# Attention decode step with an MLP on one core: unread products in TensorE's waits, half of the last matrix as 512-column products, three weight loads fewer, no VectorE branch

## The chip, the core and the metric

The kernel runs on one core of a Trainium2 chip. The metric is the device time of one execution in microseconds. Three runs of the kernel before took 190.09 to 190.26 us, with a median of 190.16 us.

## What is computed

One token goes through grouped-query attention over a cache of 16384 positions (32 query heads, 8 key/value heads, head size 128), then through a block that ends in an MLP of width 1792. The shifts that the block applies along the sequence have a sequence of length one, so `jnp.pad` and the slices leave zeros, `hs` is zero and `x1` is the block's own input.

```python
x = A_x                                            # (1, 1, 512), bfloat16 like all inputs
q = layernorm(x) @ wq                              # 512 -> 32 heads x 128
scores = einsum("bhqd,bhkd->bhqk", q, k) * 128 ** -0.5   # k, v: 8 heads, each used by 4 query heads
o = einsum("bhqk,bhkd->bhqd", softmax(scores), v)
h = x + o.reshape(1, 1, 4096) @ wo                 # 4096 -> 512
z = layernorm(h)
x1 = z                                             # z + hs, with hs = 0
h2 = h + x1 + gelu(layernorm(x1) @ w3) @ w4        # 512 -> 1792 -> 512
```

Keys and values are 32 MB each (counted in 1024s), wq and wo 4 MB each, w3 and w4 1.75 MB each: 79.17 MB in all are read from memory.

## The kernel before

**Recording and issuing.** The kernel is recorded as a list of operations for each engine (`Program.op`), with the keys that each reads and writes; `emit` turns dependences into semaphore waits and issues each engine's list. ScalarE, GpSimd and SyncE are issued in straight order by `_run`. TensorE's list is issued by `_tensor`, which turns the repeated parts (queries, keys, values of the four pairs of heads) into loops with registers and branches. Each engine works its list strictly in this order. An operation recorded with no function (`dve(None)`, `pe(None, ...)`) marks a place: there `_vector` and `_tensor` put a branch that is never taken, with a prefetch hint placed at the start of the engine's program (lines 144 and 150 for VectorE, 219 and 317 for TensorE). On TensorE the mark stands before w4's sixth chunk and carries the wait for the second half of `hcol`.

**Loads.** All large loads are issued by SyncE through one queue, at line 438, in order: wq, keys of pair 0 in two halves, values of pair 0, keys of pair 1, and so on. Each later one waits until its buffer is free. The keys of a pair go into two buffers `kb[0]` and `kb[1]`, the values into `vb`; the last pair's values are two loads. After the last keys, `kb[0]` takes wo and `kb[1]` takes w3 and w4. The constants `WO`, `W3` and `W4` cut these into separate loads, each with its own semaphore: wo into three (24, 6 and 2 of its 32 columns of blocks), w3 into two (3 and 1 of 4 chunks), w4 into four (5, 5, 3 and 1 of 14 chunks).

**One pair of heads.** VectorE transposes keys from `kb` to `kt` (line 590), TensorE multiplies them with the query (lines 601 and 607), VectorE finds the maximum (617, 618), TensorE averages it (620), ScalarE takes the exponential (628), VectorE transposes the probabilities into `pt` (632), TensorE sums the denominators (650) and multiplies 64 times with the values, 512 columns each (643), VectorE gathers the blocks into `od` (659, 662) and TensorE adds them up (665).

**The tail.** After the fourth pair, in order:

- 32 products of the attention output with wo, 512 columns each (709). The weights are 32 columns wide, so four products work side by side in four column groups of the array. Their sum in PSUM is copied to `osum` in SBUF (713), and four fp32 products with `row32` add its partitions up into the residual row (715).
- Row sums for the layernorm (487 to 499, with TensorE's product at 497); ScalarE makes `hc` (721). `hc` waits for the first piece of w3.
- 16 products with w3, 448 columns each (727); variance and the power on GpSimd (505 to 513); `xsum` (732); ScalarE's Gelu in two halves (736); VectorE transposes each half to `hcol` (740).
- One fp32 product that puts `xsum` into the output sums `n_ps` (744), then 14 chunks of w4, each as four products of 128 columns into the four partition groups of `n_ps` (751): 56 products.
- ScalarE and VectorE copy the result to `fin` (756, 758), SyncE stores it (759).

## Time and profile before

| what | value |
|---|---|
| median of three runs | 190.16 us |
| the profiled execution's own time | 190.25 us |
| its span | 188.9 us |
| mean granted TensorE clock over the span | 0.819 of full speed |
| read from memory | 79.17 MB |

The span runs from the first to the last instruction of the core; the execution's own time includes what lies around it, 1.35 us here. PE stands for TensorE's products, PEld for its weight loads, DVE for VectorE, ACT for ScalarE, POOL for GpSimd and SP for SyncE; SPq is SyncE as issuer of loads. L709 is line 709 of the kernel before. Times in a row are microseconds from the span's start; in brackets stands how long the engine was idle before the row, and what ended that wait. The columns of other views are told where they are shown.

### The profile page before, as it was taken

What the parts mean: (1) busy time and instruction counts of PE and PEld (TensorE: products, weight loads), DVE (VectorE), ACT (ScalarE), POOL (GpSimd) and SP (SyncE); (2) the same over time, 40 slices, a digit from 0 to 9 for tenths busy, and PEclk for the clock granted to TensorE, in tenths of its full rate; (3) what the DMA queues carried; (4) which work ended last, traced back from release to release, by engine and by line L of the source; (5) the groups of instructions that cost most, each with busy time, mean ns of one, the idle gap of its engine ahead of it and who ended that gap; (6) DMA issues with size and microseconds to landing.
All of it is one profiled execution on the core that took longest, in us unless ns stands there. A gap on an engine that the chain in (4) does not pass through costs nothing.

```text
span 188.9 us, 2164 instructions
## 1 busy us (share of the span) xinstructions
PE 117.9 (62%) x695; PEld 46.2 (24%) x695; DVE 115.3 (61%) x140; ACT 9.3 (5%) x16; POOL 5.9 (3%) x11
## 2 busy tenths in 40 slices
PE   1009808998176399950832999606639997185664
PEld 1003303332032134320300333202213332031232
DVE  4900699995522999945047989460269897513252
ACT  3000000000200000002000000020000000500011
POOL 1900000000000000000000000000000000000010
PEclk9999996999657669996695699965797999558675
DMA  6999999999799999997999999997999999999994
GB/s 222 444 444 444 444 444 444 444 444 444 333 444 444 444 555 444 430 402 333 416 416 444 444 444 444 444 444 333 444 444 444 444 444 409 430 409 416 416 403 184
DMA packets 3325, 79.19 MB, mean 419 GB/s; under 512 B 378, under 2 KB 508, under 8 KB 1276
## 3 DMA queue, kind: packets, MB, share of 16 engines
q1 hardware_dynamic: 3316, 79.17, 98.0%
q8 instruction: 1, 0.02, 0.0%
q10 hardware_dynamic: 8, 0.00, 0.0%
HBM read 79.17 MB, written 0.00 MB: 419 GB/s over the span
## 4 chain that ended last, share of the span: by engine, by line
DMA 66%; DVE 18%; PE 10%; issue 4%; SPq 1%; DVEq 0%
DMA kb<-in_A_k_cache_dram 45%; DVE kt L590 16%; DMA kb<-in_B_w_dram 14%; DMA vb<-in_A_wq_dram 6%; PE banks L567 5%; PE banks L607 5%; SPq L438 1%; DVE qcol L574 1%; DVE qb L581 0%; PE banks L751 0%; PE banks L601 0%; DVE xn L558 0%; DVE fin L758 0%; SPq L137 0%; DVEq L137 0%
## 5 line engine op out<-in xcount | busy, mean ns | idle before, releaser
L590 DVE STREAM_TRANSPOSE kt<-kb 128x2048 int32<-128x2048 int32 (+1 forms) x37 | 71.3, 1987 | 4.7 <-DMA kb<-in_A_k_cache_dram 3.8
L607 PE MATMUL banks<-kt,qn 128*128 x256 | 68.5, 411 | 0.5
L607 PEld LDWEIGHTS banks<-kt,qn 128*128 x256 | 26.0, 102 | 41.2 <-issue 25.4
L643 PE MATMUL banks<-vb,pt 128*32 128x512 bf16 x256 | 23.9, 555 | 3.0 <-POOLq L453 3.0
L659 DVE TENSOR_SCALAR od<-banks,rowc 128x128 f32<-128x128 f32 x4 | 1.4, 350 | 26.0 <-PE banks L643 26.0
L567 PE MATMUL banks<-vb,xn 128*128 x32 | 9.2, 461 | 9.7 <-DVE xn L558 9.7
L601 PE MATMUL banks<-qn 128*128 128x512 bf16 x8 | 3.7, 468 | 18.0 <-DVE kt L590 17.9
L632 DVE STREAM_TRANSPOSE pt<-p_sb 64x1024 bf16<-64x1024 bf16 x8 | 9.9, 1239 | 5.4 <-ACT p_sb L628 5.3
L643 PEld LDWEIGHTS banks<-vb,pt 128*32 128x32 bf16 x256 | 8.8, 134 | 16.3 <-issue 11.9
L628 ACT ACTIVATE p_sb<-banks,bias 128x1024 bf16<-128x1024 f32 x4 | 4.5, 1114 | 155.6 <-DVE nmh L624 155.6
L650 PE MATMUL banks<-acc,zd 128*32 128x1 f32 x8 | 1.1, 201 | 17.7 <-DVE pt L632 17.7
L617 DVE TENSOR_REDUCE mx<-banks 128x1 f32<-128x1024 f32 x4 | 4.9, 1224 | 8.1 <-PE banks L607 8.1
L574 DVE STREAM_TRANSPOSE qcol<-banks 64x1024 f32<-64x1024 f32 x4 | 4.8, 1227 | 7.3 <-PE banks L567 7.3
L567 PEld LDWEIGHTS banks<-vb,xn 128*128 128x128 bf16 x32 | 3.7, 115 | 14.9 <-issue 12.6
L513 POOL TENSOR_TENSOR st<-st,expo 128x1 f32<-128x1 f32 (+1 forms) x2 | 1.3, 632 | 175.8 <-DVE st L511 175.8
L620 PE MATMUL banks<-mxd,mean 128*128 128x128 f32 x8 | 2.0, 326 | 6.6 <-DVE mxd L618 6.6
L601 PEld LDWEIGHTS banks<-qn 128*128 128x128 bf16 x8 | 0.8, 99 | 20.9 <-issue 20.8
L665 PE MATMUL banks<-od,zo 128*32 128x128 f32 x8 | 1.6, 285 | 6.5 <-DVE od L662 6.5
L650 PEld LDWEIGHTS banks<-acc,zd 128*32 128x32 f32 x8 | 0.7, 138 | 18.4 <-DVE pt L632 18.4
L662 DVE SCALAR_TENSOR_TENSOR od<-banks,rowc,od 128x128 f32<-128x128 f32 x12 | 4.2, 351 | 0.4
L709 PE MATMUL banks<-kb,o_b 128*32 128x512 bf16 x32 | 3.3, 583 | 1.3 <-DMA kb<-in_A_wo_dram 1.3
L555 DVE COPY zo<-rowgh 128x32 f32<-128x32 f32 x1 | 3.6, 3630 | 0.0
(72 smaller groups left out, 43.2 us busy)
## 6 DMA issues: line engine op xcount, KB each, us to landing
kb<-in_A_k_cache_dram SPq DMA_DIRECT2D x8, 4096.0 KB, 29.4
vb<-in_A_v_cache_dram SPq DMA_DIRECT2D x2, 4096.0 KB, 29.1
vb<-in_A_wq_dram SPq DMA_DIRECT2D x1, 4096.0 KB, 12.2
kb<-in_A_wo_dram SPq DMA_DIRECT2D x1, 3072.0 KB, 27.4
kb<-in_B_w_dram SPq DMA_DIRECT2D x1, 1344.0 KB, 23.3
kb<-in_B_w_dram SPq DMA_DIRECT2D x2, 640.0 KB, 25.7
kb<-in_A_wo_dram SPq DMA_DIRECT2D x1, 768.0 KB, 28.9
kb<-in_B_w_dram SPq DMA_DIRECT2D x1, 448.0 KB, 24.0
```

The costliest lines, as they stand in the source:

```text
L555: dve(lambda e, z=z, m=m: e.tensor_copy(z[:, :].rearrange("p (n d) -> p n d", d=4), m[:, :, :].rearrange("p g h -> p (g h)").unsqueeze(2). ...
L567: pe(lambda e, k=k: e.matmul(row[:, bass.ds(P.b, 512)], copies(xn[:, k:k + 1], 128), wq_k[:, k, bass.ds(P.c, REP * DH)], start=(k == 0), s ...
L574: dve(lambda e, g=g, b=b, half=half: e.transpose(qcol[64 * g:64 * g + 64, 2 * b:2 * b + 2, :, :].rearrange("p e m u -> p (e m u)"), half.r ...
L590: P.op("DVE", lambda e, view=view: e.transpose(view(kt), view(kb[y])), r=[("r", y, i) for i in range(RPARTS)], w=[("kt", t + i) for i in r ...
L601: pe(lambda e: e.matmul(row[:, bass.ds(P.y, 512)], copies(none, 128), copies(none, 512), start=True, stop=False, skip_group_check=True), r ...
L607: pe(lambda e, n=n: e.matmul(row[:, bass.ds(P.y, 512)], qn[:, n, bass.ds(P.q, 128)], key_piece(P.k, n), start=False, stop=(n == 3), skip_g ...
L617: dve(lambda e: e.tensor_reduce(mx[:, :], s_all, AX.X, ALU.max), r=[("s", 0), ("s", 1)], w=["mx"], **both)
L628: act(lambda e: e.activation(p_sb[:, :], s_all, ACTF.Exp, bias=bias[:, 0:1], scale=float(SCALE), accum_out=acc[:, :]), r=[("s", 0), ("s", ...
L632: dve(lambda e, g=g: e.transpose(pt[64 * g:64 * g + 64, :, :, g, :], p_sb[64 * g:64 * g + 64, :]), r=["p"], w=["pt"])
L643: pe(lambda e, l=l, ct=ct, ch=ch: e.matmul(O_ps[0][32 * ct:32 * ct + 32, :], pt[:, l, ch, :, :].rearrange("p g u -> p (g u)"), tiles[:, l ...
L662: dve(lambda e, block=block, c=c: e.scalar_tensor_tensor(od[:, :], block, rowc[:, c:c + 1], od[:, :], ALU.mult, ALU.add), r=[key, "rowc", ...
L709: pe(lambda e, r_=r_, q=q: e.matmul(O_ps[0][32 * q:32 * q + 32, :], copies(o_b[:, r_:r_ + 1], 32), wo_sb[:, r_ * D:(r_ + 1) * D], start=(r ...
```

## The change

- **Unread products.** `unread(n)` records n products of 128 by 512 that read `xn` and write bank 7 of PSUM, which nothing reads afterwards. `P.spin(n)` marks the next operation of TensorE: before it (and before its waits), `_spin` puts a loop of n passes with one such product each, counted in a register that the keys' loop also uses.
- Places: a loop of 11 before the denominators' product of every pair; two products before the pair's last product (665); a loop of 8 before wo's products; one after them; two after the sums of `osum`; three before w3's products; two after them.
- **Loads.** wo is cut in two (24 and 8), w3 is one load, w4 is cut in three (7, 5 and 2 chunks). `hc` no longer waits for w3; its first product does.
- **w4.** The first seven chunks become seven products of 512 columns into the free bank `O_ps[1]`, in the four column groups like wo's. VectorE copies the sum to `osum`, and four fp32 products with `row32` add it into `n_ps`. The other seven chunks stay as they were, 28 products of 128 columns. TensorE's mark with the never-taken branch now stands between the copy and these sums, and waits for the copy.
- **VectorE's branch.** Its mark, branch, register and prefetch hint are gone.

```diff
+    def _spin(self, eng, o):
+        passes = self.spins.get(id(o))
+        if passes is None:
+            return
+        self.loops += 1
+        n = f"pe_unread{self.loops}"
+        eng.reg_mov(self.turn, 0)
+        eng.br(n)
+        self.nc.switch_bb(n, parent=None)
+        self.unread(eng)
+        eng.reg_add(self.turn, self.turn, 1)
+        eng.br_lt(self.turn, passes, n, n + "_on")
+        self.nc.switch_bb(n + "_on", parent=None)
...
     def _vector(self):
         eng = self.nc.vector
-        rv = eng.alloc_register("never")
-        hint = eng.mark_branch_hint_location()
-        eng.reg_mov(rv, 0)
         ops, seen = self.ops["DVE"], {}
-        on = next(n for n, o in enumerate(ops) if o.fn is None)
-        self._run(eng, ops[:on], seen)
-
-        eng.br_lt(rv, 0, "body", "ve_on").branch_hint(hint)
-        self.nc.switch_bb("ve_on", parent=None)
-        self._run(eng, ops[on + 1:], seen)
+        self._run(eng, ops, seen)
...
-WO = ((0, 24), (24, 30), (30, 32))
+WO = ((0, 24), (24, 32))
-W3 = ((0, 3), (3, 4))
-W4 = ((0, 5), (5, 10), (10, 13), (13, 14))
+W3 = ((0, 4),)
+W4 = ((0, 7), (7, 12), (12, 14))
...
+        P.unread = lambda e: e.matmul(banks[:, 7, :], copies(xn[:, 0:1], 128), copies(xn[:, 0:1], 512),
+                                      start=True, stop=True)
+        def unread(n):
+            for _ in range(n):
+                pe(P.unread, r=["xn"], w=["spare1"])
...
         def sums(j):
+            P.spin(11)
...
+            unread(2)
             pe(lambda e: e.matmul(A_ps[0:32, 0:128], zo[:, :], od[:, :], start=True, stop=True),
...
+        P.spin(8)
         for r_ in range(32):
...
+        unread(1)
         h_ps, hkey = banks[:, 6, :], "spare0"
...
+        unread(2)
         row_sums(1, h_ps, hkey)
+        unread(3)
         act(lambda e: e.activation(hc[:, :, :], hT[:, :, :], ACTF.Identity, bias=s[:, 0:1], scale=1.0),
-            r=["hT", (S, 0)] + [("r", 1, 0)], w=["hc"])
+            r=["hT", (S, 0)], w=["hc"])
...
+        unread(2)
         for n in range(2):
             lo, hi = n * NHC // 2, (n + 1) * NHC // 2
...
-        dve(None)
...
-        for m in range(NHC):
-            if m == W4[0][1]:
-                pe(None, r=[("hcol", 1)])
+        near = W4[0][1]
+        for m in range(near):
+            q = m % 4
+            pe(lambda e, m=m, q=q: e.matmul(O_ps[1][32 * q:32 * q + 32, :], hcol[:, m, :], w4_sb[:, m, :],
+                                            start=(m < 4), stop=(m >= near - 4)),
+               r=[("hcol", 2 * m // NHC), ("r", 1, len(W3) + piece(W4, m))], w=[("O", 1)], bank=[("O", 1)])
+        dve(lambda e: e.tensor_copy(osum[:, :], O_ps[1][:, :]), r=[("O", 1)], w=["osum"], bank=[("O", 1)])
+        pe(None, r=["osum"])
+        for o in range(4):
+            pe(lambda e, o=o: e.matmul(
+                n_ps[32 * o:32 * o + 32, 0:128], copies(row32[:, 0:1], 32),
+                osum[:, BLOCK[o] * 128:(BLOCK[o] + 1) * 128], start=False, stop=False, skip_group_check=True),
+               r=["osum", "row32"], w=["n"], bank=["mn"])
+        for m in range(near, NHC):
             for o in range(4):
```

More of the change, by code (lines that the diff above doesn't have):

```diff
@@ L42, in __init__, with spin @@
         self.y = self.q = self.k = self.b = self.c = None
+        self.unread, self.spins, self.turn, self.passes, self.loops = None, {}, None, None, 0
+    def spin(self, passes):
+        self.passes = passes
+    def _spin(self, eng, o):
[11 more added lines that the diff above has]
+        self.nc.switch_bb(n + "_on", parent=None)
     def part(self, *mark):
@@ L84, in op @@
             o.sem, o.val, o.needed = self.dma_sems[dma], self.dma_count[dma], True
+        if eng == "PE" and self.passes is not None:
+            self.spins[id(o)], self.passes = self.passes, None
         self.ops[eng].append(o)
@@ L134, in _run @@
         for o in ops:
+            self._spin(eng, o)
             for i, (s, v, _) in self._wants(o).items():
@@ L218, in _tensor @@
         r, rl, ry, rq, rk = (eng.alloc_register(n) for n in ("seen", "landed", "half", "query", "piece"))
+        self.turn = rk
         hint = eng.mark_branch_hint_location()
@@ L289, in straight @@
             for a in places(kind, 1):
+                self._spin(eng, at[a])
                 v = rest.get((kind, a[-1]))
@@ L728, in bass_sequential_preLN__gqa_block_cached__mixer_s_mlp__decode_kernel @@
                                                 w3_sb[:, k, q * FQ:(q + 1) * FQ], start=(k == 0), stop=(k == NCH - 1)),
-                   r=["hc"] + [("r", 1, n) for n in (piece(W3, k),) if n], w=[("s", 0)], bank=[("s", 0)])
+                   r=["hc", ("r", 1, piece(W3, k))], w=[("s", 0)], bank=[("s", 0)])
         variance(1)
```

## The prediction

> **What bounds the kernel now.** I read the page first (span, busy shares, memory traffic, the shares of the chain that ended last):

> ```profile
> span 188.9 us, 2164 instructions
> PE 117.9 (62%) x695; PEld 46.2 (24%) x695; DVE 115.3 (61%) x140; ACT 9.3 (5%) x16; POOL 5.9 (3%) x11
> HBM read 79.17 MB, written 0.00 MB: 419 GB/s over the span
> DMA 66%; DVE 18%; PE 10%; issue 4%; SPq 1%; DVEq 0%
> ```

> No compute engine is busy for two thirds of the span, and the chain is mostly DMA. Then the queue table for the stretch 2 to 184 us, and the table of stretches for 14 to 100 us:

> ```profile
> q1 hardware_dynamic: 2916, 77.84, 99.6%
> ```
> ```profile
> 14.00:100.00 86.00, 57.51 (x304) 22.26 (x302) 54.42 (x53) 2.41 (x4) 0.00 (x0) 0.84 1.00 433
> ```

> The one data queue fills all 16 DMA engines 99.6% of that time, at 433 GB/s: the stream of keys, values and weights never waits for compute. So a faster engine under it gains nothing, and only two things can move the end: when the stream ends, and what follows its last byte. The end of the chain of waits shows the second:

> ```profile
> 159.94 26.79 DMA kb<-in_B_w_dram
> ...
> 186.77 0.65 PE banks L751 x15
> ...
> 187.44 0.29 DVE fin L758
> ```

> These and the timeline of the tail (start, length, engine, line, count, idle time before) are the case:

> ```profile
> 160.93 0.49 PE L620 MATMUL banks<-mxd,mean 128*128 128x128 f32 x2 [1.64 <-DVE mxd L618]
> 165.84 0.26 PE L650 MATMUL banks<-acc,zd 128*32 128x1 f32 x2 [4.42 <-DVE pt L632]
> 165.93 6.49 PE L643 MATMUL banks<-vb,pt 128*32 128x512 bf16 x64
> 174.04 0.41 PE L665 MATMUL banks<-od,zo 128*32 128x128 f32 x2 [1.63 <-DVE od L662]
> 175.77 3.27 PE L709 MATMUL banks<-kb,o_b 128*32 128x512 bf16 x32 [1.32 <-DMA kb<-in_A_wo_dram]
> 179.09 0.69 DVE L713 COPY osum<-banks 128x512 f32<-128x512 f32 x1 [3.64 <-PE banks L709]
> 179.84 0.42 PE L715 MATMUL banks<-osum,row 128*32 128x128 f32 x8 [0.80 <-DVE osum L713]
> 182.09 1.69 PE L727 MATMUL banks<-kb,hc 128*32 128x448 bf16 x16 [0.69 <-ACT hc L721]
> 183.82 0.85 ACT L736 ACTIVATE hg<-banks,st 128x224 bf16<-128x224 f32 x2 [1.79 <-PE banks L727]
> 184.98 1.53 PE L751 MATMUL banks<-kb,hcol 128*32 128x128 bf16 x40 [0.48 <-DVE hcol L740]
> 186.77 0.62 PE L751 MATMUL banks<-kb,hcol 128*32 128x128 bf16 x16 [0.27 <-DMA kb<-in_B_w_dram]
> 187.79 0.33 SPq L759 DMA_DIRECT2D out_dram<-fin  x1
> ```

> From 175.77 on, TensorE keeps pace with the arriving weights and waits for them twice, the last time at 186.77. After its last product (187.39) come the final copies and the store.

> **Part 1: three weight loads fewer.** Issue rows of SyncE, and the page's time from issue to landing:

> ```profile
> 148.24 1.28 SPq L438 DMA_DIRECT2D kb<-in_A_wo_dram  x3
> 160.42 5.85 SPq L438 DMA_DIRECT2D kb<-in_B_w_dram  x1
> ```
> ```profile
> kb<-in_A_wo_dram SPq DMA_DIRECT2D x1, 3072.0 KB, 27.4
> kb<-in_B_w_dram SPq DMA_DIRECT2D x1, 1344.0 KB, 23.3
> kb<-in_B_w_dram SPq DMA_DIRECT2D x1, 128.0 KB, 26.6
> ```

> The first piece of wo is issued at 148.24 and lands 27.4 later, at 175.64. The last piece of w4 lands at 160.42 + 26.6 = 187.02. Between them 8 loads bring 4608 KB (4.72 MB): at 433 GB/s that is 10.90 us, and they took 11.38. So a load costs about 0.48 / 8 = 0.06 us beyond its bytes. The change has 5 loads there in place of 8, for the same bytes: -0.18, with 0 (all the excess lies in something other than the number of loads) and -0.48 (all of it goes) as bounds. I take -0.18, since equal shares over unequal loads are the plain reading. New landings, each by bytes / 433 + 0.06: wo 178.12, w3 182.42, first seven chunks of w4 184.60, next five 186.17, last two 186.84. SyncE's issues are no part of it: even the one that took 5.85 us was over 20 us ahead of its data.

> **Part 2: what follows the last byte.** Before, 4 products of 128 columns follow it; now 8, two rounds of four column groups. Grouped durations (min/median/max) and the pitch of weight loads that accompany 512-column products:

> ```profile
> L607 PE MATMUL banks<-kt,qn x256: 376/378/634, 29.4 to 158.9; 128*128 x128
> L751 PE MATMUL banks<-kb,hcol x56: 286/314/314, 185.0 to 187.1; 128*32 128x128 bf16 x56
> ```
> ```profile
> 14.13 0.15 PEld L567 LDWEIGHTS banks<-vb,xn 128*128 128x128 bf16 x1 [0.19 <-issue]
> 14.56 0.15 PEld L567 LDWEIGHTS banks<-vb,xn 128*128 128x128 bf16 x1 [0.28 <-issue]
> ...
> 18.28 4.20 PEld L567 LDWEIGHTS banks<-vb,xn 128*128 128x128 bf16 x20 [0.15 <-issue]
> ```

> At half clock a 512-column product follows the last by 0.43, at full clock by 4.20 / 20 = 0.21; a lone one lasts about 0.63 or 0.38. Scaled to 128 columns (an estimate) a round is 0.11 or 0.055, and a product 0.29 or 0.22. So the new ending costs 0.055 - 0.07 = -0.01 at full clock and +0.11 at half. I take -0.01, by the clock argument below.

> **Part 3: unread products.** They write a bank that nobody reads, to keep the granted clock up. Stretches of 3.41 us, the steps in which this trace's clock changes (fields: length, PE busy, PEld, DVE, ACT, POOL, clock, DMA share, GB/s):

> ```profile
> 21.56:24.97 3.41, 1.41 (x7) 0.45 (x5) 2.33 (x3) 0.00 (x0) 0.00 (x0) 1.00 1.07 461
> 93.24:96.65 3.41, 2.27 (x44) 0.86 (x36) 1.01 (x3) 0.00 (x0) 0.00 (x0) 1.00 1.01 432
> 158.09:161.50 3.41, 1.61 (x7) 0.68 (x6) 1.56 (x3) 0.00 (x0) 0.00 (x0) 1.00 0.82 356
> 161.50:164.92 3.42, 0.00 (x0) 0.00 (x0) 2.04 (x5) 2.69 (x4) 0.00 (x0) 0.50 1.06 460
> 175.16:178.57 3.41, 2.80 (x28) 1.27 (x32) 0.26 (x2) 0.00 (x0) 0.00 (x0) 0.50 1.05 426
> 178.57:181.98 3.41, 1.28 (x18) 0.46 (x10) 2.08 (x9) 0.35 (x1) 0.00 (x0) 1.00 0.99 408
> 181.98:185.40 3.42, 2.83 (x38) 1.39 (x38) 1.87 (x7) 0.91 (x3) 0.70 (x1) 0.50 1.00 406
> ```

> A busy stretch (2.80) was followed by full clock, 1.28 and 1.61 by half (161.50 shows what followed the latter), while 1.41 at 21.56 and 2.27 at 93.24 kept it: the edge for keeping it lies somewhere between 1.3 and 1.7. In the changed tail I count, per stretch, 5 to 8 unread products of 0.21 beside the real work, each burst with some 0.17 of latency: 1.7 to 2.3 busy. That should keep it, without much to spare. [...]

> The eleven passes stand in every pair's loop between L620 and L650. One pass is a product, an addition and a taken branch; the row nearest to that is the 0.43 pitch at 14.13, from a loop that branches every fourth product (bounds: 0.21, a bare product, and 0.63, one wholly exposed). Eleven take 4.7 us (2.3 to 6.9) from 161.42 and L650 is due at 165.84, 4.4 later: 0.3 late at worst by 0.43, 2.5 by 0.63. Behind L650 the 64 products of L643 (6.49 at half clock, about 3.5 at full) win it back, and the weights of wo land at 175.64 regardless. In the first three pairs the stream covers it; without that cover it would be 0.3 a pair. The eight passes before wo's products end (8 x 0.43 after about 172.4) near 175.8, just when wo is there.

> **Part 4: w4's first half through SBUF.** In order, at full clock, against the landings of part 1: wo's last two rounds from 178.17 end at 178.76 (before 179.04), so the copy L713 and all down to w3's input come 0.3 earlier, at 181.8; w3 lands only at 182.42. Its 16 products: 3 x 0.19 + 0.35 = 0.9, ended 183.39. Activation and first transpose as before (183.82 to 184.98 = 1.16): 184.60, when w4's first seven land. Seven 512-column products: 0.21 + 0.38, ended 185.23. Copy of 512 columns (0.69 by L713's row): 185.97. Wait, branch never taken, four fp32 sums (0.42 by L715's row, next ones may follow after about 0.25): 186.35. Then five rounds, 0.3: 186.65. The last chunks land at 186.84, so 0.2 us of slack remain. The branch moves ahead of these sums and now queues all later products behind the copy on VectorE; its own cost no row shows apart (0 to 0.35; I take 0.1), so the slack lies between 0.3 and nothing.

> VectorE's branch, its register and its prefetch hint go. They stand on no path here; zero, but see the second rival.

> **Sum.** -0.18 - 0.01 = -0.19 us: 190.06 for the profiled execution's 190.25, 189.97 for the median of 190.16.

> **Rivals.** (a) TensorE's clock falls to half in the tail. From the 512-column products on: they end at 185.70, the sums may start at 186.6, 28 products take 7 x 0.11 + 0.2 from 186.9, ended 187.87 against 187.39: 190.6. From w3's products on (1.69 in place of 0.9): +1.1, 191.3. It decides from the stretch that holds 182 us. For it: the 1.61 that lost the clock; against: the unread counts. (b) Without its branch VectorE's code is fetched at another moment. In 184 to 189 us one code packet moved:

> ```profile
> q8 instruction: 1, 0.02, 1.5%
> ```

> and none from 2 to 184. Put into the stream, 16 KB on one of 16 engines (433 / 16 = 27 GB/s) holds that engine's share of every later load back 0.6 us: 190.57. Against it: the packet may be another engine's. [...] (c) Fewer loads save more: all 0.48, 189.67. (d) They save nothing: 190.15.

> **How the numbers follow.** Forecast 0.50, own range 189.75 to 190.15; (a) 0.16; (b) 0.12; (c) 0.14; (d) 0.08. A measurement here tells no more than about 0.2% (0.38 us) from no change: faster means below 189.78. (c) and the forecast's edge (0.03) give 0.17; (a) and (b) 0.28; the rest 0.55. The range 189.65 to 190.65 leaves out the deeper half of (a) and the edges.

> **What would show it.** Right: last weights land near 186.85, the granted clock is 1.00 from about 165 to the end, the last products wait for a load. Wrong: 0.50 after 182 us or the last wait put down to osum (a); a code packet before 184 us and a wider spread of landings (b); landings more than 0.3 earlier (c).

## The result and the profile after

The changed kernel takes 190.61 us (median of 20 runs, 190.34 to 192.23), the kernel before beside it 190.14 us (20 runs, 189.88 to 190.64): a ratio of 1.003, with a 95% interval of 1.0018 to 1.0042. It is slower, where faster by 0.2 us was forecast. The profiled execution is one of the longer ones: it took 191.54 us, with 2.1 us outside its span in place of 1.35. From the page of its profile:

```profile
span 189.4 us, 2378 instructions
...
PEclk9999975999788559999696699979966999999999
...
q1 hardware_dynamic: 2884, 79.17, 97.5%
q14 instruction: 1, 0.01, 0.0%
...
HBM read 79.17 MB, written 0.00 MB: 418 GB/s over the span
DMA 65%; DVE 16%; PE 15%; issue 3%; ACT 0%; SPq 0%; DVEq 0%
...
L498 PE MATMUL banks<-xn 128*128 128x512 bf16 x68 | 25.2, 443 | 0.6
```

The PEclk row (40 slices of the span, tenths of full speed) ends in nine nines: the unread products (line 498 here) hold the clock in the whole tail (1.00 from 165.00 to 187.50 us; without them, told below, it is 0.50 in 182.30 to 185.70). New is the row q14: one code packet, that is, a piece of an engine's program that is fetched from memory while the kernel runs. For the stretch 2 to 184 us, where before had the data queue alone, the queue table now has two rows, and for 50 to 60 us the second is still there:

```profile
q1 hardware_dynamic: 2594, 77.97, 99.6%
q14 instruction: 1, 0.01, 0.0%
```
```profile
q14 instruction: 1, 0.01, 0.2%
```

The packet records say what it does (start, ns, queue, bytes). They name no DMA engine; the packet that starts within 6 ns of the code packet's end is taken for that engine's next. Below them stands when loads arrived on the first, the fifteenth and the last of the 16 DMA engines:

```
after: 53.630   312 q14  8192
       53.936  1869 q1  32768     the same DMA engine's next packet
       53.685  1213 q1  32768     another engine's

                            before                   after
values of pair 0      51.21  51.59  51.73     51.18  51.68  51.69
first keys of pair 1  60.93  61.31  61.44     60.89  61.41  62.34
first piece of wo    175.35 175.63 175.64    175.22 175.53 176.39
last piece of w4     186.78 187.04 187.05    186.43 186.72 187.53
```

The packet takes 0.31 us of one DMA engine and that engine's next data packet 0.66 more (1869 - 1213 ns). From then on one engine is 0.8 to 0.9 behind the other fifteen at every load to the end, and the products wait for that one: w3 is there on fifteen engines at 182.31 and on the last at 183.15, and its products start at 183.29. Fifteen engines end at 186.72, where 186.84 was forecast; the sixteenth at 187.53. The timeline of the tail:

```profile
161.94 4.25 PE L498 MATMUL banks<-xn 128*128 128x512 bf16 x11
...
166.61 1.91 PE L665 MATMUL banks<-vb,pt 128*32 128x512 bf16 x32
...
173.02 3.33 PE L498 MATMUL banks<-xn 128*128 128x512 bf16 x8
...
176.52 1.48 PE L734 MATMUL banks<-kb,o_b 128*32 128x512 bf16 x24 [0.17 <-DMA kb<-in_A_wo_dram]
...
183.29 0.94 PE L755 MATMUL banks<-kb,hc 128*32 128x448 bf16 x16 [0.74 <-DMA kb<-in_B_w_dram]
...
185.49 0.61 PE L778 MATMUL banks<-kb,hcol 128*32 128x512 bf16 x7 [0.50 <-DVE hcol L769]
186.15 0.69 DVE L781 COPY osum<-banks 128x512 f32<-128x512 f32 x1 [0.30 <-PE banks L778]
...
187.01 0.42 PE L784 MATMUL banks<-osum,row 128*32 128x128 f32 x8 [0.91 <-DVE osum L781]
...
187.24 0.63 PE L790 MATMUL banks<-kb,hcol 128*32 128x128 bf16 x28
```

The w3 products wait for their load until 183.29 (182.42 forecast), and everything behind them moves with it: the last products end at 187.87, 0.5 later than before (187.39), though they run at full clock. The granted clock by stretches (columns as in the prediction) and the end of the chain of waits, which starts from w3's late landing:

```profile
165.00:187.50 22.50, 16.27 (x184) 5.99 (x184) 8.55 (x26) 1.70 (x5) 0.70 (x1) 1.00 0.93 396
```
```profile
158.84 24.31 DMA kb<-in_B_w_dram
...
183.29 0.96 PE banks L755 x16
```

### The profile page after: what moved, and what is told of

The parts are those of the page before. It is cut to its first block, busy times and chain, and to the rows that moved or that the text cites. A ratio compares the mean times of both kernels' runs of the same rounds, so it can differ in the third digit from the quotient of the medians.

```text
span 189.4 us, 2378 instructions
## 1 busy us (share of the span) xinstructions
PE 132.3 (70%) x750; PEld 48.9 (26%) x750; DVE 116.1 (61%) x141; ACT 9.3 (5%) x16; POOL 5.9 (3%) x11
## 3 DMA queue, kind: packets, MB, share of 16 engines
q1 hardware_dynamic: 2884, 79.17, 97.5%
HBM read 79.17 MB, written 0.00 MB: 418 GB/s over the span
## 4 chain that ended last, share of the span: by engine, by line
DMA 65%; DVE 16%; PE 15%; issue 3%; ACT 0%; SPq 0%; DVEq 0%
DMA kb<-in_A_k_cache_dram 45%; DVE kt L612 14%; DMA kb<-in_B_w_dram 13%; PE banks L629 8%; DMA vb<-in_A_wq_dram 6%; PE banks L589 5%; DVE qcol L596 1%; PE banks L623 1%; PE banks L755 1%; DVE qb L603 0%; DVE osum L781 0%; PE banks L778 0%; DVE hcol L769 0%; ACT hg L765 0%; PE banks L790 0%
## 5 line engine op out<-in xcount | busy, mean ns | idle before, releaser
L629 PE MATMUL banks<-kt,qn 128*128 x256 | 69.4, 415 | 0.4
L498 PE MATMUL banks<-xn 128*128 128x512 bf16 x68 | 25.2, 443 | 0.6
L665 PE MATMUL banks<-vb,pt 128*32 128x512 bf16 x256 | 16.1, 405 | 3.6 <-POOLq L468 3.0
L589 PE MATMUL banks<-vb,xn 128*128 x32 | 9.8, 480 | 9.7 <-DVE xn L580 9.7
L650 ACT ACTIVATE p_sb<-banks,bias 128x1024 bf16<-128x1024 f32 x4 | 4.5, 1114 | 156.3 <-DVE nmh L646 156.3
L498 PEld LDWEIGHTS banks<-xn 128*128 128x128 bf16 x68 | 6.2, 100 | 17.1 <-issue 16.9
L665 PEld LDWEIGHTS banks<-vb,pt 128*32 128x32 bf16 x256 | 6.8, 102 | 11.1 <-POOLq L468 3.2
L739 DVE COPY osum<-banks 128x512 f32<-128x512 f32 x1 | 0.7, 692 | 5.5 <-PE banks L734 5.5
## 6 DMA issues: line engine op xcount, KB each, us to landing
kb<-in_A_wo_dram SPq DMA_DIRECT2D x1, 3072.0 KB, 27.4
```

The costliest lines, as they stand in the source:

```text
L498: P.unread = lambda e: e.matmul(banks[:, 7, :], copies(xn[:, 0:1], 128), copies(xn[:, 0:1], 512), start=True, stop=True)
L589: pe(lambda e, k=k: e.matmul(row[:, bass.ds(P.b, 512)], copies(xn[:, k:k + 1], 128), wq_k[:, k, bass.ds(P.c, REP * DH)], start=(k == 0), s ...
L629: pe(lambda e, n=n: e.matmul(row[:, bass.ds(P.y, 512)], qn[:, n, bass.ds(P.q, 128)], key_piece(P.k, n), start=False, stop=(n == 3), skip_g ...
L650: act(lambda e: e.activation(p_sb[:, :], s_all, ACTF.Exp, bias=bias[:, 0:1], scale=float(SCALE), accum_out=acc[:, :]), r=[("s", 0), ("s", ...
L665: pe(lambda e, l=l, ct=ct, ch=ch: e.matmul(O_ps[0][32 * ct:32 * ct + 32, :], pt[:, l, ch, :, :].rearrange("p g u -> p (g u)"), tiles[:, l ...
```

## The experiments

Theory 1: the packet is VectorE's code, fetched inside the stream because the branch with its hint is gone; this costs some 0.6 us, and the rest of the change gains what was forecast. None of the kernels below leaves out a part of the computation. Unless said otherwise, the kernel before took 190.13 to 190.21 us beside them.

**The change with VectorE's branch put back.**

```diff
 def _vector(self):
+    rv = eng.alloc_register("never")
+    hint = eng.mark_branch_hint_location()
...
+    eng.br_lt(rv, 0, "body", "ve_on").branch_hint(hint)
```

> The changed kernel with VectorE's never-taken branch and its hint put back at the old place. Theory 1 (VectorE's missing branch lets a code fetch into the stream, and moves the last code fetch behind the store): no code packet between 2 and 184 us, first and last DMA engine's landing of a load at most 0.35 us apart to the end, last weights at 186.8 to 187.0, time 189.9 to 190.0, about 0.6 below the changed kernel. Theory 2 (the code fetch is TensorE's, from the loops of unread products): the code packet near 53 us stays, landings spread by 1.1, time 190.6. Theory 3 (the loss is the copy of osum ahead of the last products): no code packet, but time still 190.4 or more.

Measured: 189.85 us (12 runs, 189.71 to 191.0). The ratio to before is 0.9995 (0.998 to 1.001): three of the twelve executions have 2.1 to 2.4 us behind (that is, outside) their span, as the profiled one of the change had. The same kernel once more:

> e1_branch_back once more. If the late branch of TensorE makes the long runs: about a quarter of its runs have 1.9 to 2.5 us behind the span in place of 1.35, median 189.85 to 189.95. If not: as many as in e6_again.

Again 189.85 (12 runs), one of them long, ratio 0.9987 (0.9977 to 0.9997). No code packet lies in the stream; the queue table of 2 to 184 us has one row, and the tail runs as forecast:

```profile
q1 hardware_dynamic: 2609, 77.98, 99.5%
```
```profile
182.39 0.94 PE L763 MATMUL banks<-kb,hc 128*32 128x448 bf16 x16 [0.73 <-DMA kb<-in_B_w_dram]
...
184.58 0.61 PE L787 MATMUL banks<-kb,hcol 128*32 128x512 bf16 x7 [0.49 <-DVE hcol L777]
186.10 0.42 PE L793 MATMUL banks<-osum,row 128*32 128x128 f32 x8 [0.91 <-DVE osum L790]
186.32 0.68 PE L799 MATMUL banks<-kb,hcol 128*32 128x128 bf16 x28
```

w3's products start at 182.39 and w4's wide ones at 184.58, against 182.42 and 184.60 in the prediction. The branch that was costed at nothing is worth 190.61 - 189.85 = 0.76 us.

**The kernel before without VectorE's branch**, and nothing else changed.

```diff
-    eng.br_lt(rv, 0, "body", "ve_on").branch_hint(hint)
...
-        dve(None)
```

> The kernel before with only VectorE's branch, register and hint taken out. Theory 1: one code packet inside the stream, landings behind it spread by about 1.1 in place of 0.3, last weights at 187.6 to 187.9, time 190.7 to 190.9. Theory 2: no code packet in the stream, time 190.1 to 190.2. Theory 3: 190.15.

Measured: 190.98 us (5 runs), ratio 1.0045 (1.0032 to 1.0058), +0.82. The packet is there, at 53.61, 309 ns, its engine's next data packet 1864 ns:

```profile
q1 hardware_dynamic: 2932, 77.93, 99.6%
q14 instruction: 1, 0.01, 0.0%
```

The last load lands at 187.71, its fifteenth engine at 186.83. So the removal alone does it, whatever the tail looks like.

**The kernel before with VectorE's mark moved** to a place between the second and the third pair.

```diff
 for j in range(PAIRS):
+    if j == 2:
+        P.part()
+        dve(None)
...
-        dve(None)
```

> The kernel before with VectorE's mark moved from the end of the tail to the place between the second and the third pair of heads. Theory 1a (the hinted branch holds the fetch of VectorE's next code back until it is passed): one code packet of 8 KB within 2 us behind the branch, near 100 us, landings spread by 1.2 from there on, 190.8 to 191.0. Theory 1b (the hint itself keeps the fetch away, wherever the branch stands): no code packet, 190.15. Theory 1c (the fetch comes at a fixed instruction): the packet at 53 us, 190.9.

Measured: 190.14 us (8 runs), ratio 0.9998 (0.9988 to 1.0008), no code packet between 2 and 184 us. The branch is reached at 98.9 us here, some 86 us earlier than in the kernel before (184.7), and still keeps the fetch away. With the branch in place the span holds no code packet but one of 16 KB near its end (186.64 in the profile before), put down to TensorE below, so the traces do not show when VectorE's later code arrives. Hint and branch were not tried apart, and why they keep the fetch away stays open.

**Without the branch, the fetch moved in the program**: 24 one-column writes on VectorE early in the kernel.

```diff
         zd = sb("zd", [128, 32], FP32)
+        pad = sb("pad", [128, 24], FP32)
...
+        for i in range(24):
+            dve(lambda e, i=i: e.memset(pad[:, i:i + 1], 0.0), w=[("pad", i)])
```

> e2_branch_gone (the kernel before without VectorE's branch) with 24 one-column writes more on VectorE at 9 to 13 us, where it waits for wq. Theory 1a (VectorE fetches its next code when it reaches a fixed place in its program; in e2_branch_gone it had just reached its 57th recorded instruction at 53.0): the 8 KB packet comes 24 instructions earlier, at 25 to 28 us, time unchanged at 190.8 to 191.1. Theory 1b (a fixed time, or another engine's progress): packet at 53 to 54 us.

Measured: the packet comes at 31.66 us, 22 us earlier, though later than the 25 to 28 expected, so it goes by VectorE's place in its program: it is VectorE's code. But the time is 189.99 us (8 runs), ratio 0.9988 (0.9978 to 0.9997): a miss, since a fetch in the stream should have cost here too. One engine did fall 0.8 behind, and was still 0.45 behind at the last load; yet that load landed at 186.91, and the eight loads behind wo's first piece took 11.18 us in place of 11.37 to 11.44. Their packets were shorter (404 ns in place of 408 for w3's first piece, 196 in place of 201 for the 640 KB pieces of w4). The new tile had moved the buffers by 96 bytes a partition (theory P: that made the loads faster). Two kernels take that apart: the kernel before with the tile alone, and the kernel with the writes, its tile behind all buffers.

```diff
         zd = sb("zd", [128, 32], FP32)
+        pad = sb("pad", [128, 24], FP32)
```

> The kernel before with one unused tile of 96 bytes a partition ahead of the buffers, as in the kernel with the earlier code fetch, whose weight loads after the first piece of wo took 11.18 us though they were eight (11.38 to 11.41 in the other kernels with eight loads), with packets of 404 ns in place of 408. Theory P (the moved buffers made those loads faster): 11.18 here too, no code packet in the stream, a time of 189.9 to 190.0, about 0.2 below the kernel before. Rival (it was the early fetch, or the instructions that moved it): 11.4 and 190.16 as before.

```diff
-        pad = sb("pad", [128, 24], FP32)
...
         kt = sb("kt", [128, 128 * DH], BF16)
+        pad = sb("pad", [128, 24], FP32)
```

> The kernel before without VectorE's branch and with 24 one-column writes on VectorE, as in the kernel with the earlier code fetch, but with the tile that they write behind all buffers, so that these keep their places. Theory P: the code packet stays near 31.7 us, the weight loads after the first piece of wo take 11.4 us again, and the time is 0.2 above that kernel's 189.99, at 190.2, plus what the lagging DMA engine then costs: 190.2 to 190.7. Rival (an early fetch costs nothing, wherever the buffers lie): 189.9 to 190.05.

Measured: the tile alone gives 189.41 us (6 runs), ratio 0.9964 (0.9952 to 0.9977), a gain of 0.7 where 0.2 was expected; 11.18 us for the eight loads. The writes without the move give 190.96 us (4 runs), ratio 1.0043 (1.0026 to 1.006), above the 190.2 to 190.7 expected; packet at 29.56 us, one engine a full 1.0 behind at the last load (186.80 and 187.82), loads again 11.39. So the fetch costs 0.8 at 30 us (190.96 - 190.13) as at 54 us, 0.6 with moved buffers (189.99 - 189.41), and the gain of the moved buffers had hidden it. The last products of the moved kernel:

```profile
185.84 0.62 PE L752 MATMUL banks<-kb,hcol 128*32 128x128 bf16 x16 [0.19 <-DMA kb<-in_B_w_dram]
```

They start at 185.84, where those of the kernel before start at 186.77 in its profiled execution, with the same loads and the same code; by the medians the gain is 0.72 (190.13 - 189.41). Some 0.2 of it lies in the eight last loads. Most of the rest was there before them, which the expectation left out: wo's first piece had landed at 174.94, where the kernels with the old place and no late engine have 175.3 to 175.7; each 4 MB ahead of it had taken 9.68 us in place of 9.70 to 9.73. Two other distances, 32 and 64 bytes, say what it is about the place:

```diff
+        pad = sb("pad", [128, 8], FP32)
```

> The kernel before with an unused tile of 32 bytes a partition ahead of the buffers. In the kernel before the buffers begin at byte 49056 of each partition (32 beyond a multiple of 64, 160 beyond a multiple of 256); 96 bytes further (49152) they begin at a multiple of 256, and the time fell to 189.41 us. Here they begin at 49088: a multiple of 64, not of 256. If a multiple of 64 is what shortens the packets: 404 ns for w3's first piece, 11.18 us for the last eight loads, 189.4 us. If it takes a multiple of 256: 408 ns, 11.4, 190.1 to 190.2.

```diff
+        pad = sb("pad", [128, 16], FP32)
```

> The kernel before with an unused tile of 64 bytes ahead of the buffers, which then begin at 49120: 32 beyond a multiple of 64, 224 beyond one of 256. If the start of the buffers decides, by 64 or by 256: no change, 408 ns, 11.4 us, 190.1 to 190.2. If any move does it (the tile shifts other small tiles, too), or the distance alone: 189.4 to 189.8.

Measured: 190.17 us (10 runs), ratio 1.0001 (0.9991 to 1.0011), and 190.22 (10 runs), ratio 1.0002 (0.9993 to 1.0012). Median packets of some sizes, with the byte of each partition at which the buffers start:

```
                  start   mod 128   5120 bytes   10752 bytes   eight last loads
kernel before     49056        32       201 ns        408 ns           11.41 us
moved by 32       49088        64       201 ns        408 ns           11.39 us
moved by 64       49120        96       201 ns      407.5 ns           11.44 us
moved by 96       49152         0       196 ns        404 ns           11.18 us
```

A multiple of 64 isn't enough (49088 is one: 190.17 us), and the move itself does nothing (190.22 us at 49120): of the four starts only 49152 gains. It is a multiple of 128, of 256 and of far more, and none of the other three is one of 128, so the runs can't tell which multiple it takes, nor why the start matters. The price is 4 to 5 ns a packet of these sizes; packets of 3584 bytes kept their median of 140 ns.

**The change without its unread products**, with VectorE's branch and without.

```diff
 def unread(n):
-    for _ in range(n):
+    for _ in range(0):
...
-            P.spin(11)
...
-        P.spin(8)
```

> VectorE's branch back, no unread products, w4 through SBUF. By the difference between e3_no_unread and the changed kernel (192.5 - 190.61 = 1.9): 191.6 to 191.9, granted clock 0.50 from w3's products on, last wait ended by the copy of osum. By the prediction's price for half clock (1.1): 190.9 to 191.1. If the unread products matter only where the code fetch delays loads: 190.1.

> The changed kernel without any unread product (neither loops nor single ones; the result is the same). Theory 1: the code packet stays in the stream, the granted clock is 0.50 in most of the tail, time 191.0 to 191.7. Theory 2: no code packet in the stream, landings spread by 0.3, but the half clock in the tail: 190.6 to 191.3. Theory 3: the copy comes later still, 191 or more.

Measured: 191.58 us with the branch (4 runs), ratio 1.0076 (1.0061 to 1.0091), and 192.5 without it (4 runs), ratio 1.012 (1.0104 to 1.0135). The kernel with the branch, by stretches and by the timeline:

```profile
178.90:182.30 3.40, 1.11 (x18) 0.46 (x10) 2.20 (x10) 0.40 (x1) 0.00 (x0) 1.00 0.98 411
182.30:185.70 3.40, 2.68 (x22) 1.17 (x25) 1.59 (x6) 0.85 (x2) 0.71 (x1) 0.50 0.98 398
```
```profile
182.55 1.69 PE L761 MATMUL banks<-kb,hc 128*32 128x448 bf16 x16 [0.99 <-DMA kb<-in_B_w_dram]
...
187.80 0.99 PE L797 MATMUL banks<-kb,hcol 128*32 128x128 bf16 x28
```

After a stretch with 1.11 us busy the clock is 0.50, w3's products take 1.69 in place of 0.94, and the last products end at 188.79 though their weights landed at 186.80: rival (a) at its place, with a higher price (191.3 was forecast). Two of the four executions without the branch are long ones, with 2.1 and 2.4 us behind the span; the other two took 192.12 and 192.19. From that stretch up to w3's products TensorE was idle for 0.99 at most (the first of the last two rows). The longest idle time does not sort the cases: in the profile before, the stretch of 178.57 us lost the clock with none over 0.80, and that of 21.56 kept it with one of 2.00. Busy time per stretch sorts them better, though not sharply. Of the full-clock stretches of 3.41 us in all traces of this case, none with under 1.4 us busy kept the clock (the 1.41 at 21.56 us in the prediction is the least that did). The busiest that lost it had 2.40, most of it unread products (86.18 to 89.59 us in the kernel with TensorE's mark moved, told below). Between these it went both ways.

**The kernel before with the load cuts alone** (TensorE's mark then stands ahead of the eighth chunk, and, as in the change, the products with w3 wait for w3 in place of `hc`).

```diff
-WO = ((0, 24), (24, 30), (30, 32))
+WO = ((0, 24), (24, 32))
-W3 = ((0, 3), (3, 4))
-W4 = ((0, 5), (5, 10), (10, 13), (13, 14))
+W3 = ((0, 4),)
+W4 = ((0, 7), (7, 12), (12, 14))
```

> The kernel before with only the cuts of wo, w3 and w4 of the changed kernel (three loads fewer; the products unchanged; TensorE's branch now stands before w4's eighth chunk). By the prediction's price of 0.06 a load: last weights 0.18 earlier than before, time 189.95 to 190.05. If the excess belongs to something other than the number of loads: 190.15. If two chunks behind the last byte at half clock cost more: up to 190.25.

Measured: 190.08 us (12 runs), ratio 1.0002 (0.9991 to 1.0014): no change that can be told, and a little above the 189.95 to 190.05 expected. Its loads take 11.17 us from wo's first landing to the last one, before's 11.41: -0.24. Part 2 of the prediction had +0.11 of that given back at half clock, which this kernel has in its tail (0.50 in 182.30 to 185.70).

**The change with its branch back, but w4 in 128-column products** as before, TensorE's mark ahead of the eighth chunk.

```diff
-        near = W4[0][1]
-        for m in range(near):
...
-        for m in range(near, NHC):
+        for m in range(NHC):
+            if m == W4[0][1]:
+                pe(None, r=[("hcol", 1)])
```

> VectorE's branch back, unread products and three loads fewer kept, but all 14 chunks of w4 as 128-column products as before, with TensorE's branch ahead of the eighth chunk. Theory 1 (with a full clock everything after w3 waits for the landings, so the 512-column products through SBUF are worth nothing): 189.75 to 189.95, TensorE's last wait ended by a load. Rival (the wide products carry the gain): 190.1 or more.

Measured: 191.91 us (4 runs), ratio 1.0098 (1.0083 to 1.0114), 2 us above what was expected. The last rows of TensorE:

```profile
186.14 0.46 PE L788 MATMUL banks<-kb,hcol 128*32 128x128 bf16 x20 [0.94 <-DMA kb<-in_B_w_dram]
188.59 0.30 PE L788 MATMUL banks<-kb,hcol 128*32 128x128 bf16 x8 [1.99 <-issue]
```

The last weights landed at 186.71, and TensorE waited for nothing that the profile shows until 188.59. A code packet of 16 KB ran from 186.21 for 0.96 us. The pages of the kernel with wide products (the branch put back, first row) and of this one (second row) count TensorE's products and weight loads:

```profile
PE 130.2 (69%) x745; PEld 49.0 (26%) x750; DVE 116.1 (62%) x141; ACT 9.3 (5%) x16; POOL 5.9 (3%) x11
```
```profile
PE 132.8 (70%) x758; PEld 49.5 (26%) x763; DVE 115.4 (61%) x140; ACT 9.3 (5%) x16; POOL 5.9 (3%) x11
```

The narrow way is 13 products and 13 weight loads longer, and the unread products had lengthened the program already: its last 8 products with their loads, 16 instructions, would lie in the piece of code (those 16 KB) that TensorE doesn't have yet. The kernel with eight more unread products, told below, puts that reading to the test.

**The change with its branch back, TensorE's mark ahead of the wait for the copy**: the branch is reached at 184.86 us in place of 185.96.

```diff
-        pe(None, r=["osum"])
+        pe(None, r=[("hcol", 1)])
```

> VectorE's branch back (as in e1_branch_back) and TensorE's branch moved: it waits for the second half of hcol and stands ahead of the wait for the copy of osum. Theory 1 (some runs of e1_branch_back are 0.8 to 1.1 longer behind the span because TensorE's last code block is fetched only after the store when its branch comes late): branch near 185.0, 16 KB code packet about 1.2 later, time less span at most 1.5 in every run, median 189.8 to 189.9, no run above 190.4. Rival (the long runs have nothing to do with the branch): a fifth of the runs stay at 190.7 to 191.1. Second rival (the packet now falls into the last load): last weights 0.5 to 1.0 later than in e1_branch_back, 190.3 to 190.9.

> e6_mark_early once more, beside e1_again on the same chip. If the late branch of TensorE makes the long runs: no run of this one with more than 1.6 us behind its span, median 189.85 to 189.95. If not: as many as in e1_again.

Measured: 189.94 (11 runs), ratio 0.9987 (0.9978 to 0.9996), and 189.93 (11 runs), ratio 0.9985 (0.9977 to 0.9994). None of its 22 executions has more than 1.49 us behind the span. The sums wait less after the copy, 0.79 in place of 0.91:

```profile
185.85 0.42 PE L793 MATMUL banks<-osum,row 128*32 128x128 f32 x8 [0.79 <-DVE osum L790]
186.09 0.79 PE L799 MATMUL banks<-kb,hcol 128*32 128x128 bf16 x28
```

The same kernel with eight more unread products, 16 instructions, that fall into waits:

```diff
-        unread(1)
+        unread(5)
...
-        unread(3)
+        unread(7)
```

> e6_mark_early with eight more unread products: five in place of one behind wo's products, seven in place of three ahead of w3's. Theory 1 (TensorE's code reaches the edge of a block within the last products, as in e8_narrow_w4, where 26 more instructions than in e6_mark_early stopped it ahead of its last 8 products; 16 more leave about three products behind the edge): the last products stand until about 188.4, put down to issue, time 191.4 to 192.0. Rival (the stop in e8_narrow_w4 comes from the 128-column products of w4, not from the code's length): 189.9 to 190.1, all added products hidden behind the copy of osum and w3's load.

Measured: 192.24 us (2 runs, 191.97 and 192.51), ratio 1.0106 (1.0088 to 1.0125), a little above the 191.4 to 192.0 expected. The last products come in two groups:

```profile
186.58 0.55 PE L799 MATMUL banks<-kb,hcol 128*32 128x128 bf16 x25
188.86 0.24 PE L799 MATMUL banks<-kb,hcol 128*32 128x128 bf16 x3 [1.73 <-issue]
```

TensorE stands 1.7 us ahead of three products, 6 instructions with their weight loads. With 16 added and 6 behind the edge, the kernel without the addition ends 10 ahead of it; the narrow way, 26 longer, had to have 16 behind it, and has. That shows the edge, and how little room the change leaves.

**The fastest kernel with the buffers moved** by the unused tile.

> The fastest kernel so far (VectorE's branch back, TensorE's branch ahead of the wait for the copy) with the unused tile of 96 bytes ahead of the buffers. Theory P: its five loads after the first piece of wo take about 11.0 in place of 11.18, but the chain through w3, the copy and the sums ends only 0.1 to 0.2 earlier with them, 189.75 to 189.85 (189.93 without the tile). Rival: 189.93.

Measured: 189.30 us (4 runs), ratio 0.9957 (0.994 to 0.9973), the fastest of all; 0.6 below the same kernel without the tile, more than expected. Its loads behind wo's first piece take 11.04 us (11.18 without the tile), and wo's first piece lands 0.3 to 0.5 earlier (175.02; 175.35 and 175.56 in the two profiles without the tile). With the buffers moved, little is left of the change itself: 189.30 beside 189.41 for the kernel before with the same tile, and the intervals of the two ratios overlap.

## Why the prediction was wrong, by its steps

**The step that failed** is the last sentence on part 4: VectorE's branch, register and hint "stand on no path here; zero". Their removal costs 0.76 to 0.82 us. It is rival (b), with its place (a code packet inside the stream, one DMA engine behind for the rest) and nearly its size. That its 190.57 lies beside the 190.61 measured is luck in part: the +0.6 stood for 16 KB at one engine's rate, but 8 KB came, which took 0.31 us, and the other 0.66 is a delay of the next packet that no part of the prediction had. The 16 KB packet on which the figure rested is, by its place, TensorE's, as the prediction feared: it comes 1.2 us behind TensorE's never-taken branch (185.43 and 186.64 in the profile before), and near the end of every other trace it follows that branch, too. Rival (b) was given a chance of 0.12. What spoke against it was that the profile before showed no code packet between 2 and 184 us. That row had to be read the other way round: VectorE works through nearly all its 140 instructions there with no fetch in 180 us, and a hint that is placed at the program's start; the thing removed could be the reason that the row was empty. In a stream that fills the DMA engines 99.6% of the time no run here hid the fetch of 8 KB: where its cost can be read against the same kernel without it, it is 0.58 to 0.83 us.

**The stream as bound**: right. The loss inside the span is landings some 0.8 late, carried by w3's products to the end.

**Part 1, three loads fewer**: right in the landings; the load cuts alone moved the time by no more than the noise. Forecast 11.20 us from wo's first landing to the last (175.64 to 186.84); 11.14 to 11.19 in every kernel with five loads in the old place, 11.37 to 11.44 with eight. With moved buffers eight take 11.18 and five 11.04: 0.14 to 0.24 for three loads, where 0.18 was taken.

**Part 2, the ending**: right. From the last landing to the last product's end it is 0.34 before (187.05 to 187.39) and 0.34 in the kernel with TensorE's mark moved (186.54 to 186.88).

**Part 3, the clock**: right in its outcome, 1.00 in the whole tail. Its edge, "somewhere between 1.3 and 1.7" us busy, is not borne out: stretches with up to 2.40 lost the clock elsewhere. Eleven passes took 4.25 us (4.7 forecast), eight ended at 176.35 (175.8 forecast), both without harm. That the change needs them is shown by the kernels without them: +1.7 to +1.9 against the same kernel with them (191.58 to 189.85, 192.5 to 190.61), where rival (a) had 191.3 in all. This is their worth beside the wide products of w4, not their worth to the kernel before. With the load cuts and both branches kept, neither of the two gives 190.08 us, wide products alone 191.58, unread products alone 191.91, and both together 189.85: each alone does harm (the second by the stop in TensorE's code), and the pair is worth some 0.2, little more than the noise.

**Part 4, the way through SBUF**: right in its times. With VectorE's branch back the sums start at 186.10 and in the change at 187.01, both ahead of the last landing (186.66 and 187.53). The branch between copy and sums costs 0.12 (0.91 - 0.79), where 0.1 was taken. What the prediction missed is another worth of the wide products: they shorten the program.

**The sum** of all but the failed step was -0.19. The change with the branch back has -0.31 (189.85 to 190.16), with TensorE's mark moved -0.23 to -0.27. So the rest of the change gained about 0.1 more than the forecast. With the price of the failed step taken from the kernel before, where it was measured by itself, -0.31 + 0.82 makes +0.51; +0.47 was measured.

**What is shown and what is not.** That the missing branch puts VectorE's code packet into the stream, and its price, is shown in both directions and at two places. Not shown is why the branch or its hint keeps the fetch out, and why the next data packet takes 0.66 us longer. That the long executions (over 1.9 us behind the span: 4 of 20 of the change, 4 of 24 with the branch back, 2 of 4 without unread products, 1 of 12 with the load cuts alone, none of 22 with TensorE's mark moved and none of the kernel before) come from TensorE's last 16 KB of code is only likely: in the three profiled long ones that packet starts 3.9 to 4.4 us behind TensorE's branch, when the store has already been issued, and 1.1 to 1.8 us behind it in the others. Against a late branch as the whole reason stands the kernel with the branch and without unread products: its branch comes at 187.25, later than in the change (186.88), and none of its four executions is long.

## What to carry to other kernels

In this kernel, whose stream fills the DMA engines 99.6% of the time, the branch that kept a code fetch out of it was worth 0.76 to 0.82 us, though no row of the profile names it: before removing a branch or a hint, ask which empty row it is the cause of, and look for a code packet in the queue table afterwards. One DMA engine of 16 that fell behind was 0.8 to 0.9 us late in the change for every load that followed, so compare the arrival on the fifteenth engine with that on the last. Count instructions to the end of the program as well as time (16 more made 189.94 us into 192.24), and where a stream is the bound, look at which byte of a partition its buffers start: here a tile in front of them was worth 0.72 us, more than the change under test (0.31 with its branch back).
